# Ninety-seven half-width operand sums on GpSimd instead of VectorE, in a kernel that is planned instruction by instruction

## The chip, the cores and the metric

The kernel runs on one core of a Trainium2 chip. The metric is device time in microseconds (us). The kernel before was timed three times: 1730.5, 1730.49 and 1730.0 us, with a median of 1730.49 us.

The core has a TensorE (PE in the profile, and PEld for its weight loads), a VectorE (DVE), a ScalarE (ACT), a GpSimd (POOL) and a SyncE (SP). In this kernel SP issues nearly all loads, and POOL issues nearly all stores and all transfers that add to what is already at their destination.

## The reference

Two branches are computed from inputs of 2048 rows and mixed by a gate that has one value for each row:

```python
g = sigmoid((x * gate_w).sum(-1, keepdims=True))           # x: 2048 x 1024
a = einsum("bsd,ed->bse", x, dft_hid_re)                   # 1024 x 1024 matrices
b = einsum("bsd,ed->bse", x, dft_hid_im)
A = einsum("ts,bse->bte", dft_seq_re, a) - einsum("ts,bse->bte", dft_seq_im, b)   # 2048 x 2048 matrices
h = einsum("bsd,df->bsf", x, w1) + b1                      # 1024 -> 3584
r = where(h > 0, h, 0); r = r * r
B = einsum("bsf,fd->bsd", r, w2) + b2                      # 3584 -> 1024
out = g * A + (1 - g) * B
```

Everything is 32-bit floating point. The kernel takes `A_x` as the x of both branches, as the reference does.

## The kernel before

**Stages.** The work is five matrix products in order: the x stage (x with the two hidden matrices, giving a and b, called `ab`), the c stage (the two sequence matrices with `ab`, giving the first branch, times the gate), two h stages (x with the two parts of w1, then bias, relu and square), and the o stage (the squares with w2, bias, gate and the sum of both branches). What goes from one stage to the next is stored to device memory and loaded again.

**Fewer products.** Each product is split into 2 x 2 blocks and formed by the Winograd scheme: seven block products in place of eight, at the price of sums of blocks. The sums are listed in `SUMS_L` and `SUMS_R` (S1 to S4 of the left, T1 to T4 of the right operand, lines 63 to 77). For the block products named in `TWICE_X`, `TWICE_C`, `TWICE_O` and `TWICE_H` the scheme is applied a second time. The sums of operands are tiles called `raw` (made in the place of a loaded block) or `sum`; tiles called `u`, `y`, `h`, `ab` and `o` hold results. Block results are combined from PSUM, mostly by VectorE instructions that read one operand from PSUM (`ps`).

**Precision.** Each operand is split into a high part `hi`, which ScalarE makes by a copy to TensorE's reduced 32-bit type, and a low part `lo`, which VectorE makes by subtraction. Each pair of tiles is multiplied three times: hi with hi, hi with lo, lo with hi. A tile named `both` holds the two parts of a narrow operand side by side. For operands marked in `MINUS_C` and `MINUS_O` ScalarE makes a negated copy instead, and an adding DMA from POOL makes `lo` of it.

**Sums by DMA.** For some sums, chosen by the `LAND_...`, `LAND2_...` and `APART_...` tables, the second block is added to the first by an adding DMA, so that VectorE does nothing. `SHARE2`, `MADE`, `LOW` and `HIGH` say which sums, low parts and high parts are stored to be loaded by a later use, `EARLY_...` and `NOW_...` which are made ahead of their use, `NOT_OUT` which outputs of the first branch are kept aside and not written to the output at once.

**The planner.** Nothing is issued while the kernel is described. Every instruction is recorded as an `Op` (line 134) with the engine, the operands and a modelled time, for instance `VEC[0] + VEC[1] * n` for VectorE. `plan` (line 1458) then plays the program on modelled engines and queues. The matmuls have a fixed order. Every other instruction has a due time, worked back from the matmul that needs it, and whenever a modelled engine is idle, it takes the instruction that is due first among those whose inputs are there. A tile gets one of 55 slots when its turn comes; the turn is its due time less a lead, `LEAD` and `LEADS`, where `LEADS` is a table of corrections for each 25 us of the program. `emit` (line 1610) issues everything in the order so found, and ties the instructions of each engine to that order; so all instructions stand under line 1628 of the profile, and they are told apart by their tiles' names. Waits between engines follow from the data. An `Op` can also have a `gate`, an instruction whose end it has to wait for though it needs nothing from it; before the change only some DMAs of POOL have one (lines 1566 to 1571).

The heart of the choice, for any engine other than TensorE (lines 1562 to 1564):

```python
                if not ready[e]:
                    continue
                op = ready[e][0][2]
```

## Time and profile before

| | |
|---|---|
| median of three runs | 1730.49 us |
| span of the profiled execution, first to last instruction | 1727.9 us |
| what lies around the span, against the median | 2.6 us |
| TensorE busy, instructions | 1722.6 us (100%), 8024 |
| TensorE weight loads busy | 1508.7 us (87%), 8024 |
| VectorE busy, instructions | 1658.3 us (96%), 1659 |
| ScalarE busy, instructions | 1151.2 us (67%), 1296 |
| GpSimd busy, instructions | 284.3 us (16%), 413 |
| moved by DMA | 559.89 MB |
| DMA engines' time taken by SP's and ACT's packets, by POOL's packets | 52.9%, 44.4% |

The profile is of one execution. A row of a group gives the line, the engine, the operation, the tile written and those read, the shapes and the count; then the busy time in us and the mean of one in ns; then the idle time ahead of the group and what ended most of it. In rows of the timeline the first number is the start, the second the length, in us. In rows of waits stand the total, the number of times and the longest. POOL's busy time before the change is the issuing of DMAs, with four small memsets at the start.

### The profile page before, as it was taken

To read this page: it belongs to the slowest core of one execution; us is meant where nothing else is said; L and a number is where in the kernel's file an instruction comes from. 1 tells how busy PE (TensorE), PEld (TensorE's weight loads), DVE (VectorE), ACT (ScalarE), POOL (GpSimd) and SP (SyncE) were. 2 spreads that over 40 slices of the span, in tenths; PEclk is the share of its full clock that TensorE was granted. 3 is DMA by queue.
4 is the path that set the end of the run, shared out by engine and by line. 5 is a ranking of instruction groups with operands and counts; after the bars stand their busy time and mean duration, and the time that the engine had idled before them with its cause. 6 is when DMAs were issued, how large, how long until landed. Compare 5 with 4: busy or idle time off the path is not lost.

```text
span 1727.9 us, 22479 instructions
## 1 busy us (share of the span) xinstructions
PE 1722.6 (100%) x8024; PEld 1508.7 (87%) x8024; DVE 1658.3 (96%) x1659; ACT 1151.2 (67%) x1296; POOL 284.3 (16%) x413
## 2 busy tenths in 40 slices
PE   9999999999999999999999999999999999999999
PEld 8888888888888888888888888888888888888888
DVE  7999999999999899899999999999999999899997
ACT  5475565874675675466595668987897666476673
POOL 1212221111211100121121210101211120111131
PEclk9999999999999999999999999999999999999999
DMA  9996999999999999998998999999999999999997
GB/s 347 365 375 259 322 387 343 292 285 327 285 307 352 291 310 399 323 295 285 371 359 311 276 355 344 351 379 358 309 345 324 336 272 381 341 277 334 334 295 162
DMA packets 157807, 559.89 MB, mean 324 GB/s; under 512 B 17776, under 2 KB 18304, under 8 KB 157696
## 3 DMA queue, kind: packets, MB, share of 16 engines
q1 hardware_dynamic: 98352, 351.07, 52.9%
q0 software_dynamic: 58912, 207.00, 44.4%
q8 instruction: 63, 1.03, 0.2%
q10 hardware_dynamic: 432, 0.39, 0.1%
q14 instruction: 48, 0.39, 0.1%
HBM read 390.09 MB, written 134.75 MB: 304 GB/s over the span
## 4 chain that ended last, share of the span: by engine, by line
PE 96%; DVE 3%; DMA 1%; issue 0%; ACT 0%; DVEq 0%; POOLq 0%
PE ps L1628 96%; DVE lo L1628 1%; DVE sum L1628 1%; DMA raw<-in_w1a 1%; DVE y L1628 0%; DVE both L1628 0%; DVE u L1628 0%; DVE raw L1628 0%; ACT hi L1628 0%; ACT y L1628 0%; DVE o L1628 0%; ACT both L1628 0%; ACT ps L1628 0%; DVE ones L1628 0%; DVEq L1628 0%
## 5 line engine op out<-in xcount | busy, mean ns | idle before, releaser
L1628 PE MATMUL ps<-hi,lo 128*128 128x512 f32 (+1 forms) x2100 | 730.4, 378 | 0.1
L1628 PE MATMUL ps<-hi 128*128 128x512 f32 (+1 forms) x2100 | 730.4, 378 | 0.0
L1628 PE MATMUL ps<-lo,hi 128*128 128x512 f32 (+1 forms) x2100 | 730.3, 378 | 0.0
L1628 ACT ACTIVATE hi<-raw 128x1024 fp32r<-128x1024 f32 (+2 forms) x397 | 401.5, 1032 | 200.2 <-DVE raw L1628 79.6
L1628 PEld LDWEIGHTS ps<-hi,lo 128*128 128x128 f32 x2100 | 396.6, 189 | 56.5 <-DVE lo L1628 0.7
L1628 PEld LDWEIGHTS ps<-lo,hi 128*128 128x128 f32 x2100 | 396.7, 189 | 56.1 <-DVE lo L1628 0.2
L1628 PEld LDWEIGHTS ps<-hi 128*128 128x128 f32 x2100 | 396.6, 189 | 56.0 <-ACT hi L1628 0.2
L1628 DVE TENSOR_TENSOR lo<-raw,hi 128x1024 fp32r<-128x1024 f32 (+2 forms) x337 | 396.0, 1192 | 14.2 <-ACT hi L1628 10.8
L1628 ACT ACTIVATE hi<-sum 128x1024 fp32r<-128x1024 f32 (+1 forms) x263 | 269.1, 1032 | 136.7 <-DVE sum L1628 88.1
L1628 PE MATMUL ps<-hi,both 128*128 128x512 f32 x1120 | 312.3, 379 | 0.0
L1628 DVE TENSOR_TENSOR lo<-sum,hi 128x1024 fp32r<-128x1024 f32 (+1 forms) x230 | 270.5, 1191 | 8.7 <-PE ps L1628 4.6
L1628 PEld LDWEIGHTS ps<-hi,both 128*128 128x128 f32 x1120 | 211.7, 189 | 30.2 <-ACT ps L1628 0.2
L1628 DVE TENSOR_TENSOR raw<-raw 128x1024 f32<-128x1024 f32 (+1 forms) x175 | 205.7, 1195 | 1.6 <-DMA raw<-in_ct 0.5
L1628 DVE TENSOR_TENSOR sum<-raw 128x1024 f32<-128x1024 f32 (+2 forms) x182 | 180.5, 1002 | 7.9 <-PE ps L1628 4.4
L1628 PE MATMUL ps<-lo,both 128*128 128x512 f32 x560 | 182.9, 379 | 0.0
L1628 DVE TENSOR_TENSOR sum<-raw,sum 128x1024 f32<-128x1024 f32 (+2 forms) x139 | 147.6, 1066 | 4.4 <-DMA raw<-copy 2.1
L1628 ACT ACTIVATE u<-ps 128x1024 f32<-128x1024 f32 (+1 forms) x91 | 88.1, 970 | 47.5 <-PE ps L1628 28.0
L1628 PEld LDWEIGHTS ps<-lo,both 128*128 128x128 f32 x560 | 105.8, 189 | 15.0
L1628 ACT ACTIVATE ps<-u 128x1024 f32<-128x1024 f32 (+1 forms) x69 | 67.8, 987 | 21.9 <-DVE u L1628 9.5
L1628 POOL DMA_DIRECT2D h<-h x58 | 31.3, 542 | 250.5 <-ACT h L1628 91.0
L1628 POOL DMA_DIRECT2D lo<-raw x38 | 34.0, 896 | 224.9 <-ACT lo L1628 172.1
L1628 ACT ACTIVATE both<-sum 128x512 fp32r<-128x512 f32 x68 | 42.3, 622 | 35.9 <-DVE sum L1628 33.7
(87 smaller groups left out, 1140.0 us busy)
## 6 DMA issues: line engine op xcount, KB each, us to landing
raw<-in_ct SPq DMA_DIRECT2D x137, 512.0 KB, 10.1
raw<-h SPq DMA_DIRECT2D x99, 512.0 KB, 10.5
raw<-in_w SPq DMA_DIRECT2D x90, 512.0 KB, 10.3
raw<-ab SPq DMA_DIRECT2D x72, 512.0 KB, 10.9
raw<-copy SPq DMA_DIRECT2D x65, 512.0 KB, 7.8
raw<-in_x SPq DMA_DIRECT2D x56, 512.0 KB, 8.4
copy<-raw POOLq DMA_DIRECT2D x48, 512.0 KB, 6.9
h<-h POOLq DMA_DIRECT2D x44, 512.0 KB, 6.6
```

What stands on the lines that cost most here:

```text
L1628: made = getattr(real[op.engine], op.name)(*(actual(a) for a in op.args), **{k: actual(v) for k, v in op.kwargs.items()})
```

## The change

Of the operand sums that VectorE would make, 97 half-width ones (128 x 512) are issued on GpSimd. A sum that is 512 wide goes as a whole. A sum that is 1024 wide is cut into two halves; one goes to GpSimd, the other is left to VectorE, or goes to GpSimd at a later occasion.

Which sums go is decided in `plan`. VectorE's ready instructions are kept in two heaps: those with more than one operand in SBUF (and `tensor_scalar`), flagged `two`, and the others, in `single`, which are mostly those that read PSUM. Whenever VectorE begins one of the `single` kind, `beside` looks for a sum to be put on GpSimd at that moment. It wants GpSimd idle, no POOL instruction ready that is due within 2 us, an instruction on VectorE about as long as the modelled sum (0.1 + 2.2e-3 x 512 us), and a sum whose inputs have all landed and which is due 3 us later or more. While the sum runs in the model, VectorE is given `single` instructions only. The sum gets a `gate`: the VectorE instruction just before the covering one, or the one ahead of that where the three follow each other without a pause.

Besides, the plan is made anew: the tables that say which sums are landed by DMA, kept, shared or made early have other entries, and `LEADS` has corrections in nearly every window. The tables of products (`TWICE_...`, `WIDE`, `TALL_...`, `FIRST_...`, `SPILL`) are the same, written on lines of their own.

```diff
-LAND_X, LAND_C, LAND_H, LAND_O = {'T1': 3, 'T3': 4, 'T4': 3}, {'T1': 15, 'T3': 0, 'T4': 13}, ({'T1': 0, 'T3': 4, 'T4': 3}, {'T1': 0, 'T3': 1, 'T4': 1}), {'T1': 10, 'T3': 3, 'T4': 9}
+LAND_X = {'T1': 2, 'T3': 1, 'T4': 3}
+LAND_C = {'T1': 16, 'T3': 1, 'T4': 14}
+LAND_H = ({'T1': 0, 'T3': 4, 'T4': 4}, {'T1': 0, 'T3': 1, 'T4': 3})
+LAND_O = {'T1': 10, 'T3': 3, 'T4': 9}
...
+LAND2_C = {1: {'T1': 0}, 2: {'T1': 4, 'T3': 2}, 3: {'T3': 1}, 4: {'T1': 2, 'T3': 2}, 5: {'T1': 1}, 6: {'T1': 1, 'T3': 2}, 7: {'T1': 1, 'T3': 3}}
+LAND2_O = {1: {'T1': 1, 'T3': 0}, 2: {'T1': 1}, 3: {'T3': 4, 'T1': 1}, 4: {'T3': 1}, 5: {'T1': 3, 'T3': 2}, 6: {'T1': 3}, 7: {'T1': 3, 'T3': 4}}
...
+BESIDE = (0.1, 2.2e-3, 0.05)
+BESIDE_LEAD = 3.0
+BESIDE_OVER = 0.15
+BESIDE_DMA = 2.0
...
+            near = [a for a in args[1:] if isinstance(a, Sight) and a.base.home != "bank" and a.size() >= 256]
+            self.two = engine == "vector" and (len(near) > 1 or name == "tensor_scalar")
+            self.moves = (name == "tensor_tensor" and len(near) == 2 and outs[0].base.name in ("raw", "sum")
+                          and n in (512, 1024))
...
+    single, port, recent = [], [0.0], deque([None, None], 2)
+
     def able(op):
         if op.engine != "tensor":
-            heappush(ready[op.engine], (op.due, op.at, op))
+            heappush(single if op.engine == "vector" and not op.two else ready[op.engine], (op.due, op.at, op))
+
+    def beside(t, op):
+
+        room = op.time + BESIDE_OVER
+        if (idle["gpsimd"] > t + 1e-9 or port[0] > t + 1e-9 or BESIDE[0] + BESIDE[1] * 512 > room
+                or ready["gpsimd"] and ready["gpsimd"][0][0] < t + BESIDE_DMA):
+            return
+        e = min((e for e in ready["vector"] if e[2].moves and not e[2].unlanded and e[0] >= t + BESIDE_LEAD),
+                key=lambda e: e[:2], default=None)
+        if e is None:
+            return
+        ready["vector"].remove(e)
+        heapify(ready["vector"])
+        o, time = e[2], BESIDE[0] + BESIDE[1] * 512
+        if o.whole:
+            part = o
+            part.engine, part.time = "gpsimd", time
+        else:
+            o.parts, o.moved, o.start = 2 if o.n == 1024 else 1, True, t
+            part = Beside(o, 0 if o.n == 1024 else None, "gpsimd", time, VEC_END)
+            if o.n == 1024:
+                heappush(ready["vector"], (o.due, o.at, Beside(o, 1, "vector", VEC[0] + VEC[1] * 512, VEC_END)))
+        last, before = recent[1], recent[0]
+        part.gate = before if last and before and last.start - before.start < before.time + 1e-6 and (
+            op.start - last.start < last.time + 1e-6) else last
+        part.start = t
+        order.append(part)
+        idle["gpsimd"], port[0] = t + time, t + time + BESIDE[2]
...
+            elif e == "vector":
+                heaps = [h for h in ((single,) if port[0] > t + 1e-9 else (ready[e], single)) if h]
...
+            if e == "vector":
+                if not op.two:
+                    beside(t, op)
+                recent.append(op)
```

## The prediction

> **What bounds the kernel now.** I read the page first, then how the matmuls follow each other, then what TensorE's weight loads waited for, and only then VectorE, whose work the change takes away. From the page, the span, the engines, the granted clock and the chain of waits by engine:

> ```profile
> span 1727.9 us, 22479 instructions
> PE 1722.6 (100%) x8024; PEld 1508.7 (87%) x8024; DVE 1658.3 (96%) x1659; ACT 1151.2 (67%) x1296; POOL 284.3 (16%) x413
> PEclk9999999999999999999999999999999999999999
> PE 96%; DVE 3%; DMA 1%; issue 0%; ACT 0%; DVEq 0%; POOLq 0%
> ```

> TensorE is busy for the whole span at its full granted clock, and the chain that ended last is 96% TensorE. Its busy time alone proves little, since matmuls overlap; their starts prove more. Two places of the timeline, the first real matmuls and a run near the end, with the last matmul and the work after it:

> ```profile
> 5.69 0.70 PE L1628 MATMUL ps<-hi 128*128 128x512 f32 x2
> ...
> 1718.41 0.38 PE L1628 MATMUL ps<-hi 128*128 128x512 f32 x1
> ...
> 1720.57 0.38 PE L1628 MATMUL ps<-lo,hi 128*128 128x512 f32 x1
> ...
> 1723.57 0.28 PE L1628 MATMUL ps<-hi,lo 128*128 128x256 f32 x1
> 1723.88 0.48 DVE L1628 SCALAR_TENSOR_TENSOR o<-ps,b2c,g 128x256 f32<-128x256 f32 x1 [0.34 <-PE ps L1628]
> 1724.40 0.43 DVE L1628 TENSOR_TENSOR o<-o,raw 128x256 f32<-128x256 f32 x1
> ```

> From 1718.41 to 1720.57 lie ten starts: 0.216 us each. Of the 8024 matmuls 44 are the warm-up of the code, so 7980 are real, nearly all of them 512 wide. They start between 5.69 and 1723.57 us: 1717.9 us, 0.2153 us for each, which is the pace itself. So there is hardly a hole. The waits of the weight loads say how large the holes are:

> ```profile
> PEld ps L1628 <- DVE lo L1628: 0.9, 3, 0.5
> PEld ps L1628 <- ACT ps L1628: 0.2, 1, 0.2
> PEld ps L1628 <- ACT hi L1628: 0.2, 1, 0.2
> ```

> Together 1.3 us in the whole run. The span is 5.7 us of start, 1717.9 us of matmuls and 4.3 us of tail; 1.3 us of it is waiting. VectorE, at 96%, looks like a second bound, and in some stretches it has no idle time at all:

> ```profile
> 850.00:900.00 50.00, 50.00 (x233) 43.78 (x232) 49.93 (x45) 38.44 (x46) 10.80 (x21) 1.00 0.95 364
> 900.00:950.00 50.00, 50.00 (x234) 43.77 (x233) 50.00 (x45) 28.58 (x29) 7.32 (x13) 1.00 0.89 327
> 950.00:1000.00 50.00, 50.00 (x233) 43.80 (x232) 50.00 (x45) 35.73 (x43) 14.16 (x21) 1.00 0.98 290
> 1000.00:1050.00 50.00, 50.00 (x233) 43.77 (x233) 50.00 (x46) 28.52 (x32) 3.06 (x6) 1.00 0.99 358
> ```

> The columns are the stretch, its length, busy time (with the count) of PE, PEld, DVE, ACT and POOL, the clock, the DMA share and GB/s. Over these 200 us VectorE is busy for 199.93, and yet TensorE starts as many matmuls as anywhere: VectorE works ahead of need. Its load is full without being late.

> **The change part by part.** *The matmuls.* The diff leaves alone which products are formed one level or two levels deep, their orders and the tile shapes, so the 7980 matmuls and their 1717.9 us stay. What the change can give back is at most the 1.3 us of waits: 0 to 1.3 us, and I take 0.2, since nothing says that the three waits on `lo` come from sums.

> *Sums taken from VectorE.* The rows by form of the sums and of the instructions that are to cover them:

> ```profile
> L1628 DVE TENSOR_TENSOR raw<-raw 128x1024 f32<-128x1024 f32 x160 | 191.4, 1218 | 1.6 <-DMA raw<-in_ct 0.5 <-DMA raw<-in_w 0.5 <-DMA raw<-ab 0.2
> L1628 DVE TENSOR_TENSOR sum<-raw 128x512 f32<-128x512 f32 x68 | 46.4, 685 | 3.9 <-PE ps L1628 3.6
> L1628 DVE TENSOR_TENSOR lo<-raw,hi 128x1024 fp32r<-128x1024 f32 x310 | 372.7, 1219 | 9.2 <-ACT hi L1628 5.9 <-PE ps L1628 2.4
> L1628 DVE TENSOR_TENSOR u<-u,ps 128x1024 f32<-128x1024 f32 x45 | 54.5, 1215 | 2.0 <-ACT u L1628 1.0 <-PE ps L1628 0.3
> L1628 DVE TENSOR_TENSOR h<-h,ps 128x1024 f32<-128x1024 f32 x43 | 52.2, 1214 | 1.2 <-PE ps L1628 1.0
> L1628 DVE TENSOR_TENSOR ab<-ab,ps 128x1024 f32<-128x1024 f32 x41 | 49.7, 1215 | 2.6 <-PE ps L1628 1.4 <-ACT u L1628 1.2
> ```

> A sum that is 512 wide leaves VectorE whole: 0.685 us. Of a 1024-wide one VectorE keeps a half: 1.218 - 0.685 = 0.533 us saved. For 97 halves that is 97 x 0.533 = 52 to 97 x 0.685 = 66 us; I take 60. Covers there are enough: the last three rows alone hold 129 full-width instructions that read PSUM, for 97 sums.

> *The same sums on GpSimd.* No GpSimd arithmetic is in this trace, so its price is bounded. It isn't below VectorE's own 0.685 us for that size. As the upper bound I take twice VectorE's full-width row, 2.44 us. The longest kind of instruction that GpSimd issues now is the first row here:

> ```profile
> L1628 POOL DMA_DIRECT2D out<-o x15 | 16.7, 1202 | 44.5 <-DVE o L1628 12.5 <-ACT lo L1628 11.9 <-DVE lo L1628 6.6
> L1628 POOL DMA_DIRECT2D lo<-raw x38 | 34.0, 896 | 224.9 <-ACT lo L1628 172.1 <-DVE lo L1628 19.9 <-DVE u L1628 18.0
> ```

> Between the ends I take 1.2 us, by that nearest row and because the planner puts a sum beside one full-width instruction (1.215 us). Then POOL gets 97 x 1.2 = 116 us more and is busy for 400 of 1728 us, 23%; with 2.44 us it would be 521 us, 30%. It doesn't become a bound. [...]

> *What a sum collides with.* While a sum runs over the end of its cover, the next VectorE instruction may have to wait. Nothing in this trace shows how much: POOL issued DMAs all through, and VectorE's two-SBUF-input rows (1.218 and 1.219 us) are as long as those that read PSUM (1.214 and 1.215 us), so issuing doesn't hurt it, but issuing isn't arithmetic. From below nothing, from above each sum stops VectorE for its whole 1.2 us: 116 us. I take a quarter of it, 0.3 us for each sum, 29 us, because the start of each sum hangs on a semaphore of VectorE and is off by parts of a microsecond and not by whole instructions. [...]

> *What planning anew moves.* By the tables of the diff: four fewer sums of the first stage are landed by adding DMAs (+4 VectorE instructions), three more of the second stage are (-3); one level deeper three fewer there and five more in the last stage (+3, -5); `lo` made by a negated copy and an adding DMA in five more places and in two fewer (-5, +2). That is about -4 instructions of 1.22 us. The other tables (kept operands, sums and outputs kept far, early sums) I bound by ten instructions either way: -5 us, from -17 to +7. As many adding DMAs of 0.9 us come to or leave POOL. VectorE thus ends at 1658 - 60 + 29 - 5 = 1622 us, with bounds of 1575 and 1729: only at the upper end does it become the bound.

> *Queues.* The 97 sums stand in order in POOL's queue between its some 409 DMA issues; each also waits there for its cover's turn. The issue behind it is late by at most that wait and the sum, 1.2 + 1.2 = 2.4 us. What waits for these issues are `lo<-raw` and landings, which took about 9 us before and are asked for well ahead. SP's queue gets loads in another order at the same sizes. At nothing these are costed because of the slack that the full stretches above show; without it each would be a wait of TensorE.

> The sum: 5.7 + 1717.9 + 4.3 - 0.2 = 1727.7 us of span. The median of the runs, 1730.49 us, lies 2.6 us above the profiled span; with that, **1730.3 us**. Other arithmetic at the new places may leave a wait here or there; its own range is 1729.2 to 1732.

> **The rivals.** *Contention makes VectorE the bound* (slower). Mechanism: a sum overhangs its cover and holds up VectorE's next instruction for 1.2 us while only 0.53 to 0.69 was saved, a net loss of about 0.6. It decides where VectorE has no idle time: 200 us out of 1728 hold about 11 of 97 sums, 11 x 0.6 = 7 us lost, and TensorE stands once the lead is spent. Time: 1737. For it: the full stretches. Against it: only overhangs count, and those stretches run without any wait now.

> *POOL's DMAs come late* (slower). The one larger hole now, at the change of stage, shows the mechanism; the chain of waits there:

> ```profile
> 815.91 9.39 DMA raw<-in_w1a
> 825.30 0.02 issue
> 825.32 1.06 ACT hi L1628
> 826.38 0.02 issue
> 826.41 1.24 DVE lo L1628
> 827.64 0.04 issue
> 827.69 896.17 PE ps L1628 x4174
> ```

> A transfer issued at 815.91 landed 9.39 us later, and the operand was ready 12 us after the issue, just too late. Where POOL issues such a transfer behind a sum it comes 2.4 us later; two such places without slack cost 4.8 us: 1735.3. It decides from the second such place on.

> *The change does not relieve VectorE* (it waits as long as it saves): 1730.5, since TensorE doesn't need the relief.

> [...]

> *Faster by over 0.2%* would need 3.5 us, and the waits are 1.3; only start and tail could give the rest, and no edit makes their work smaller.

> **How the numbers follow.** What a measurement tells from no change is 0.2%, 3.5 us, so 1727.0 to 1733.9 counts as the same. Chances: the forecast 0.64; no relief 0.07; first-use cost 0.03 (all the same: 0.74); POOL late 0.14 and contention 0.10 (slower: 0.24); faster 0.02. The range goes from 1729.2, below which only a shorter start could lie, up to 1737.0, the priced end of both slower cases; beyond it I leave about 0.1.

> **What would show it.** Right: the same 7980 matmuls at 0.216 us, waits of the weight loads of 0 to 3 us in sum, VectorE's busy time near 1622 us, POOL's near 400, and sum rows on POOL of about 1.2 us. Contention right: means of VectorE's two-input rows above 1.25 us. POOL late: weight loads that wait for `lo` or `hi` behind a DMA that POOL issued. The prediction is wrong if the weight loads' waits sum to over 4 us, or if the matmuls' pace is another.

## The result, and the profile after

The changed kernel takes **1742.63 us** (median of four runs, 1739.05 to 1743.09) against 1730.3 us before (median of four runs, one more than when the prediction was made): 1.0068 of the time, 95% interval 1.0054 to 1.0081. It is slower by 12.3 us, where 1730.3 us was forecast, and it lies 5.6 us above the upper end of the range. The profiled execution is the shortest of the four (1739.05 us, span 1737.3); the size of the waits differs from one execution to the next, as a second profile below shows.

From the page of the kernel after, the span, the engines, the granted clock and the chain of waits by engine:

```profile
span 1737.3 us, 22640 instructions
...
PE 1724.2 (99%) x8024; PEld 1507.6 (87%) x8024; DVE 1616.1 (93%) x1619; ACT 1148.8 (66%) x1293; POOL 445.5 (26%) x510
...
PEclk9999999999999999999999999999999999999999
...
PE 77%; DVE 3%; DMA 2%; issue 1%; ACT 1%; POOL 0%; DVEq 0%; ACTq 0%; POOLq 0%
```

VectorE did lose its work: 1658.3 us became 1616.1. The matmuls are the same 8024. What changed is the last line: TensorE's share of the chain that sets the end fell from 96% to 77%, and no other engine took it over as a bound. The chain is now broken in many places. What the weight loads waited for, kernel after (total, times, longest; a start-up row left out):

```profile
PEld ps L1741 <- DVE ab L1741: 5.3, 4, 2.3
PEld ps L1741 <- ACT ps L1741: 3.3, 5, 1.2
PEld ps L1741 <- DMA lo<-raw: 2.2, 1, 2.2
...
PEld ps L1741 <- ACT hi L1741: 0.6, 1, 0.6
PEld ps L1741 <- DVE lo L1741: 0.2, 1, 0.2
```

Together 11.6 us in twelve waits, where it was 1.3 us in five. The span grew by 9.4 us, the waits by 10.3: in the profiled execution the waits are the whole loss, to within a microsecond. GpSimd is in none of the rows. So the next question is what made VectorE, ScalarE and the adding transfer late. VectorE's own waits, kernel after:

```profile
DVE raw L1741 <- DMA raw<-in_x: 11.3, 3, 4.5
DVE sum L1741 <- DMA raw<-copy: 9.3, 5, 2.8
...
DVE raw L1741 <- DMA raw<-in_w: 5.9, 3, 3.1
```

and the largest rows of the same kind in the kernel before:

```profile
DVE sum L1628 <- DMA raw<-copy: 3.1, 4, 1.8
...
DVE sum L1628 <- DMA raw<-in_x: 1.2, 1, 1.2
```

Over all its rows VectorE waited 51.2 us for transfers after, and 6.5 us before. It has 42 us less to do and yet is later where it counts, because what it is to work on isn't there.

**One place, followed back.** The timeline of after around the first of the larger waits, from POOL's transfers to TensorE (start, length; in brackets the idle time before and what ended it):

```profile
28.54 0.85 POOL L1741 DMA_DIRECT2D raw<-in_w  x1 [8.40 <-ACT hi L1741]
...
32.10 5.33 SPq L1741 DMA_DIRECT2D raw<-in_x  x4
...
32.78 0.83 POOL L1741 DMA_DIRECT2D lo<-lo  x1
...
43.35 1.23 DVE L1741 TENSOR_TENSOR raw<-raw 128x1024 f32<-128x1024 f32 x1 [4.45 <-DMA raw<-in_x]
49.38 1.22 DVE L1741 TENSOR_TENSOR raw<-raw 128x1024 f32<-128x1024 f32 x1 [3.67 <-DMA raw<-in_x]
...
57.49 2.18 POOL L1741 TENSOR_TENSOR sum<-raw 128x512 f32<-128x512 f32 x1 [1.50 <-DVE ab L1741]
58.47 1.21 DVE L1741 TENSOR_TENSOR ab<-u,ps 128x1024 f32<-128x1024 f32 x1
...
59.74 0.48 PE L1741 MATMUL ps<-hi 128*128 128x512 f32 x1 [1.89 <-DVE ab L1741]
```

Between 28.54 and 32.78 us POOL issues eight transfers in a row (before, two in the same 5 us and the next ones at 35.91 us and later). SP's loads of x are issued into that. The first, issued at 32.10, landed at 40.75: 8.66 us, where the planner had reckoned with 6.92. The second, whose landing at 43.27 ended VectorE's first wait, took 10.75 us (planner: 9.19), and the fourth, whose landing at 49.26 ended its second wait, 12.62 us (planner: 11.49); the first and the fourth were also issued 1.4 us later than planned. POOL's eight, on the other hand, landed up to 2.9 us sooner than planned. VectorE stood 4.45 and then 3.67 us, got to `ab` late, and TensorE, which needs the PSUM bank that `ab` frees, stood 2.3 us. The first sum on GpSimd starts at 57.49, when VectorE's waits are over and the last matmul ahead of the hole has started (57.47): at this place the sums can't be the cause. In the last stage the chain of waits of after shows the same kind of thing (start, length):

```profile
1468.30 0.55 POOL copy L1741
1468.85 0.64 issue
1469.50 11.95 DMA lo<-raw
1481.50 76.29 PE ps L1741 x352
```

An adding transfer took 11.95 us (planner: 9.39) and the matmuls waited for its landing.

### The profile page after: what moved, and what is told of

It reads as the page before. It is cut to its first block, busy times and chain, and to the rows that moved or that the text cites. A ratio compares the mean times of both kernels' runs of the same rounds, so it can differ in the third digit from the quotient of the medians.

```text
span 1737.3 us, 22640 instructions
## 1 busy us (share of the span) xinstructions
PE 1724.2 (99%) x8024; PEld 1507.6 (87%) x8024; DVE 1616.1 (93%) x1619; ACT 1148.8 (66%) x1293; POOL 445.5 (26%) x510
## 4 chain that ended last, share of the span: by engine, by line
PE 77%; DVE 3%; DMA 2%; issue 1%; ACT 1%; POOL 0%; DVEq 0%; ACTq 0%; POOLq 0%
PE ps L1741 77%; DVE lo L1741 1%; DMA raw<-h 1%; DMA lo<-raw 1%; DVE raw L1741 1%; DVE u L1741 1%; DVE o L1741 1%; DVE sum L1741 0%; DMA raw<-in_w 0%; ACT ps L1741 0%; ACT hi L1741 0%; DVE both L1741 0%; ACT o L1741 0%; DVE y L1741 0%; DVE ab L1741 0%
## 5 line engine op out<-in xcount | busy, mean ns | idle before, releaser
L1741 ACT ACTIVATE hi<-raw 128x1024 fp32r<-128x1024 f32 (+2 forms) x401 | 406.3, 1032 | 193.7 <-DVE raw L1741 66.6
L1741 DVE TENSOR_TENSOR lo<-raw,hi 128x1024 fp32r<-128x1024 f32 (+2 forms) x340 | 400.5, 1192 | 24.3 <-ACT hi L1741 16.1
L1741 ACT ACTIVATE hi<-sum 128x1024 fp32r<-128x1024 f32 (+1 forms) x260 | 264.1, 1031 | 114.0 <-DVE sum L1741 62.8
L1741 DVE TENSOR_TENSOR raw<-raw 128x1024 f32<-128x1024 f32 (+2 forms) x165 | 189.5, 1159 | 27.1 <-DMA raw<-in_x 11.3
L1741 DVE TENSOR_TENSOR sum<-raw 128x512 f32<-128x512 f32 (+2 forms) x166 | 158.7, 965 | 13.9 <-DMA raw<-copy 6.8
L1741 DVE TENSOR_TENSOR sum<-raw,sum 128x1024 f32<-128x1024 f32 (+2 forms) x121 | 127.6, 1057 | 9.2 <-DMA raw<-copy 2.5
L1741 POOL TENSOR_TENSOR sum<-raw 128x512 f32<-128x512 f32 x37 | 65.8, 1778 | 101.9 <-DVE lo L1741 39.3
L1741 POOL TENSOR_TENSOR raw<-raw 128x512 f32<-128x512 f32 x33 | 54.1, 1638 | 113.0 <-DVE lo L1741 52.4
```

What stands on the lines that cost most here:

```text
L1741: made = getattr(real[op.engine], op.name)(*(actual(a) for a in op.args), **{k: actual(v) for k, v in op.kwargs.items()})
```

## The experiments

Two theories at first. **S**: the sums on GpSimd cost the time themselves, by holding up VectorE or POOL's queue. **P**: the new order of the instructions, which came with the other tables and with the planner that knows of the sums, is what loses. All ratios are to the kernel before, measured on the same chip (the first row is from the chip of after; on the others its median was 1729.7 to 1730.0 us). The waits are those of one profiled execution, which for after is the shortest of four and for after_lead the longest.

| kernel | median us | ratio, 95% interval | weight loads' waits, us (times) | VectorE's waits for DMA, us |
|---|---|---|---|---|
| before | 1730.3 | | 1.3 (5) | 6.5 |
| after | 1742.63 | 1.0068 (1.0054 to 1.0081) | 11.6 (12) | 51.2 |
| narrow_sums | 1739.85 | 1.0058 (1.0043 to 1.0073) | 8.4 (7) | 44.3 |
| extra_sums | 1729.88 | 1.0001 (0.9992 to 1.0010) | 1.0 (4) | 7.5 |
| new_order | 1740.12 | 1.0054 (1.0040 to 1.0069) | 8.2 (10) | 14.0 |
| no_sums | 1764.17 | 1.0200 (1.0183 to 1.0217) | 34.3 (34) | 28.8 |
| small_adds | 1733.85 | 1.0021 (1.0012 to 1.0031) | 4.7 (6) | 18.8 |
| old_tables | 1736.47 | 1.0037 (1.0024 to 1.0050) | 8.4 (10) | 34.3 |
| same_order | 1729.29 | 0.9997 (0.9988 to 1.0005) | 0.6 (2) | 10.4 |
| after_again | 1743.50 | 1.0078 (1.0062 to 1.0093) | 14.8 (11) | 46.7 |
| after_lead | 1750.47 | 1.0129 (1.0104 to 1.0154) | 23.9 (17) | 45.0 |
| old_leads | 1739.65 | 1.0067 (1.0050 to 1.0083) | 11.0 (15) | 37.8 |
| few_loads | 1729.69 | 1.0000 (0.9991 to 1.0009) | 2.3 (6) | 12.2 |
| more_loads | 1730.62 | 1.0006 (0.9997 to 1.0016) | 1.8 (7) | 11.2 |

The planner also gives its own account of how long it expects TensorE to stand; where that is used below it is called the account.

**narrow_sums: after's order, most of each sum left out.**

```diff
+            if op.engine == "gpsimd" and op.name == "tensor_tensor":
+                if op.outs[0].base.name == "sum":
+                    tc.nc.gpsimd.memset(args[0][..., 16:], 0.0)
+                args = [a[..., :16] for a in args]
```

> Changed kernel, same order of every engine, but each of the 97 GpSimd sums adds 16 columns and not 512 (where the sum's tile is new, the other columns are filled with zeros by GpSimd); so most of each sum is left out. Theory S (the sums themselves cost the time: their length, the collisions with VectorE and the delay of POOL's queue): the waits of the weight loads fall from 11.6 us to 3 or less, 1731 us, at most 1733. Theory P (the order that was planned anew leaves too little room where transfers land later than the planner assumed, and the sums have little to do with it): the same places of waiting, 1737 us or more.

Measured: 1739.85 us. A sum shrank to about a third, and the waits stayed. With the zeros that fill the rest of 64 new tiles (35 us), GpSimd's work for the sums fell from 166 to 96 us. The largest group of sums on POOL, and then the waits of the weight loads:

```profile
L1746 POOL TENSOR_TENSOR raw<-raw 128x16 f32<-128x16 f32 x33 | 19.0, 575 | 134.1 <-DVE lo L1746 61.3 <-DVE sum L1746 23.8 <-DVE u L1746 20.6
```

```profile
PEld ps L1746 <- ACT ps L1746: 3.3, 4, 1.4
PEld ps L1746 <- DVE ab L1746: 2.9, 2, 2.4
PEld ps L1746 <- DMA lo<-raw: 2.2, 1, 2.2
```

Of the 12.3 us some 2 to 3 came back, no more than the intervals of the two ratios leave open. Of after's three largest waits those near 58 and 1479 us stand as they stood. The third, 1.8 us near 273 us, where VectorE has no pause, fell to 0.5: about 1 us there goes with the sums. The rest speaks for P.

**extra_sums: before's order, with useless sums.** 151 sums of 320 columns on a tile that nothing else reads, each beside a VectorE instruction that reads PSUM.

```diff
+            made = tc.nc.gpsimd.tensor_tensor(extra, extra, extra, op=ADD)   # waits like a sum with a gate
```

> Kernel before, order untouched, with 151 useless sums of 320 columns on GpSimd (as many elements as 94 of 512), each beside a VectorE instruction that reads PSUM and gated as in the change. VectorE loses nothing and gains nothing but the collisions. Theory S: 1736 us or more. Theory P: 1730 to 1732.

Measured: 1729.88 us, no change. The page's engines, and the group on POOL:

```profile
PE 1722.3 (100%) x8024; PEld 1508.5 (87%) x8024; DVE 1659.5 (96%) x1660; ACT 1151.9 (67%) x1296; POOL 486.2 (28%) x564
```

```profile
L1667 POOL TENSOR_TENSOR extra<-extra 128x320 f32<-128x320 f32 x151 | 203.9, 1351 | 324.0 <-DVE lo L1651 131.0 <-DVE sum L1651 73.2 <-DVE raw L1651 39.0
```

204 us of arithmetic on GpSimd, more than the 166 us of the real sums, cost VectorE 1.2 us of busy time (1658.3 before, 1659.5 here) and TensorE nothing. Placed beside VectorE instructions that read PSUM, these 151 sums held up hardly anything; in before's order S has no mechanism left.

**new_order: before, planned anew, no sums at all.** One number of the planner's leads is other, so that the order is another while the work is the same.

```diff
-LEAD = {'hi': 2.2, 'out': 1.4, 'raw': 6.7, 'sum': 10.0}
+LEAD = {'hi': 2.5, 'out': 1.4, 'raw': 6.7, 'sum': 10.0}
```

> Kernel before, no sum on GpSimd, planned with a lead of 2.5 us in place of 2.2 for the tiles of high parts: nothing but the order of instructions and the slots differ from 468 us on. By the planner's own account its last matmul ends 1.6 us later than before. Theory S: 1730 to 1733, as the planner has it. Theory P (a new order meets late transfers that the old one happened to avoid): 1735 to 1742.

Measured: 1740.12 us, as slow as after, without one sum on GpSimd. But here the account says so itself: 7.2 us of standing against 8.2 measured. Before is the odd one: its account says 5.6, and the chip shows 1.3. So an order under the old tables need only do what its account says to lose several us against before. After's order has an account of zero and stands for 11.6 us; "any new order loses" is not yet the answer for it.

**no_sums: after's tables and planner, nothing moved.** `beside` returns at once.

```diff
     def beside(t, op):
+        return
```

> Changed kernel with its new tables, but no sum is moved to GpSimd: VectorE makes all of them. By the planner's own account TensorE then stands for 24.7 us, where with the sums moved it has 0. Theory S: the sums cost 9 us on the chip and save much less than planned, so 1745 or less. Theory P: the sums' relief is real under these tables and the new order's own 9 us come on top, 1750 to 1760.

Measured: 1764.17 us, with 34.3 us of waits; VectorE is busy for 1660.5 us. That is 4 us above P's range. Under the new tables the sums on GpSimd, with the order that goes with them, are thus worth 21.5 us. The relief is real where the plan needs it; before's plan doesn't.

**small_adds: after's order, adding transfers of a quarter of the columns.** It leaves all else in place, and takes 64 of 560 MB away.

```diff
+        if op.load and "accum_op" in op.kwargs:
+            args = [a[..., :a.shape[-1] // 4] for a in args]
```

> Changed kernel, same order of every engine and all 97 sums whole, but every adding DMA moves a quarter of its columns, so three quarters of these additions are left out. Transfers land earlier: these and the loads that share the DMA engines with them. Theory P (late landings stop TensorE): the waits of the weight loads fall from 11.6 us to 3 or less, 1731 to 1733 us. Against it, a theory O (the order is bad in itself, VectorE and ScalarE meet their due times too late whatever lands when): 1737 us or more.

Measured: 1733.85 us and 4.7 us of waits, close to P's range (1731 to 1733, 3 us or less) but outside it. Waits of the weight loads:

```profile
PEld ps L1744 <- DVE ab L1744: 3.0, 4, 1.3
...
PEld ps L1744 <- ACT hi L1744: 0.9, 1, 0.9
PEld ps L1744 <- DMA lo<-raw: 0.8, 1, 0.8
```

By the ratios some 8 of the 12 us came back by nothing but lighter transfers, with all 97 sums in full. After's loss hangs on when transfers land. It doesn't follow that they land later there than in before: in small_adds SP's loads take on average 3.4 us less than the planner reckons, sooner than in either kernel.

**old_tables: after's planner and sums (87 of them), before's tables and leads.**

```diff
-LAND_X = {'T1': 2, 'T3': 1, 'T4': 3}
+LAND_X = {'T1': 3, 'T3': 4, 'T4': 3}
...
```

> The changed planner, so sums go to GpSimd, with all tables and leads of the kernel before: the part of the change that is the sums alone (87 of them by its plan). The planner's own account ends the matmuls 3.7 us later than that of the kernel before. Theory P: a new order, so slower than its account, 1735 to 1743. Theory S (already weak): the sums' own price, 1740 or more.

Measured: 1736.47 us and 8.4 us of waits, against an account of 9.3. Under the old tables new_order and this run do what the planner says, without sums and with them.

**same_order: before's order and tables, and 57 sums moved in place.** The first halves of 40 sums 1024 wide and 17 whole ones 512 wide go to GpSimd behind a cover; nothing else is moved.

```diff
+LEAST = 1.2
...
-    for op in order:
+    for op in beside(order):     # 40 Half pieces and 17 whole sums are issued on GpSimd, with a gate
```

> The kernel before with its tables and its order kept, and 57 of its operand sums moved to GpSimd beside VectorE's instructions that read PSUM, gated as in the change: 40 halves of 1024-wide sums and 17 whole ones of 512, chosen among those whose inputs land early enough. Everything else keeps its place. Theory P: 1729 to 1731, since nothing lands later and VectorE wasn't the bound; VectorE's busy time falls by 40 x 0.53 + 17 x 0.69 = 33 us to about 1626. Theory S: 1734 or more. If relief of VectorE alone were worth time: 1728 or less.

Measured: 1729.29 us, the same time within 0.2%. The page's engines, and the weight loads' waits:

```profile
PE 1722.3 (100%) x8024; PEld 1509.0 (87%) x8024; DVE 1637.5 (95%) x1642; ACT 1150.7 (67%) x1296; POOL 387.3 (22%) x470
```

```profile
PEld ps L1674 <- ACT hi L1674: 0.4, 1, 0.4
PEld ps L1674 <- ACT ps L1674: 0.2, 1, 0.2
```

VectorE loses 20.8 us, where 33 were expected; nine of its instructions that begin inside a sum are longer, by 5.6 us in all, and the rest of the difference isn't explained. The waits fall to 0.6, and there is no more to gain, because there was no more than 1.3 us of waiting. This is what the forecast described, minus the planning anew.

**stalls_long and stalls_short: what a wait of TensorE costs.** In before's order, sums on GpSimd hold one matmul back: 8 places with three chained sums, or 16 with one.

```diff
+PLACES, SUMS = 8, 3          # stalls_short: 16, 1
...
+            tc.add_manual_dep(made.ins, idle.ins.name, ...)   # the matmul waits for the last sum
```

> Kernel before, order untouched; at 8 places, some 190 us apart and with POOL idle, one matmul waits for three chained GpSimd sums of 320 columns, which begin when the matmul ahead of it ends: 8 waits of some 3 us. If a wait costs its own length and no more: 1730 + 24 = 1754. If the granted clock is halved after such a wait, as it was for 3.4 us after a wait of 2.2 us in the kernel with narrow sums: up to 1.7 to 3.4 us more for each, 1760 to 1780.

> The same with 16 places and one sum at each: 16 waits of some 1.2 us. With or without a rule of the clock, if it asks for a longer wait than this: 1730 + 19 = 1749, and no stretch at half clock. If waits of 1.2 us are enough to halve the clock: 1755 or more.

Measured: 1788.17 us (1.0348, interval 1.0316 to 1.0381) and 1786.49 us (1.0335, 1.0302 to 1.0368), for these waits, stalls_long first and stalls_short below:

```profile
PEld ps L1643 <- POOL extra L1649: 43.3, 8, 8.5
```

```profile
PEld ps L1643 <- POOL extra L1649: 48.2, 16, 9.1
```

The waits came out longer than meant, 43.3 us for 24 and 48.2 us for 19, so both times lie above the sums of the expectations; that stalls_short passed 1755 us doesn't mean that waits of 1.2 us halve the clock. 58 us lost for 43 us of waits, 56 for 48: in these two runs nothing of the waits was made good, and 15 and 8 us were lost on top of them. What those are is in the last section.

**after_again, after_lead, old_leads: is only the fitted order off?** Two forms of P are left. **Y**: under the new tables transfers land later than the planner reckons, whatever the order. **Z**: only the one order that was fitted until its account came to zero is off, having been chosen for the planner's mistakes. The first run repeats after; the second gives it the lead of new_order; the third gives it before's table `LEADS` (99 sums).

```diff
-LEAD = {'hi': 2.2, 'out': 1.4, 'raw': 6.7, 'sum': 10.0}
+LEAD = {'hi': 2.5, 'out': 1.4, 'raw': 6.7, 'sum': 10.0}       # after_lead
-LEADS = {'hi': {0: -1.5, 1: -6.0, ...
+LEADS = {'hi': {3: -5.5, 4: -4.5, ...                         # old_leads
```

> The changed kernel once more. Its profiled run took 1739.05 us and its timed runs 1742.2 to 1743.1. If the difference is a stretch at half the granted clock behind the wait of 2.3 us near 58 us: a run of 1742 to 1743 has 6.8 us of half clock in its records (3.4 us lost), one of 1739 has none. If it is something else: the clock is whole in both.

> Changed kernel, planned with a lead of 2.5 us in place of 2.2 for the tiles of high parts: its tables, another order, 90 sums moved. By the planner's own account TensorE stands for 12.2 us (the changed kernel: 0). Theory Z (the account is about right for an order that wasn't fitted to it, and too good for the one that was): waits of the weight loads of 9 to 16 us, 1739 to 1748 us with some half clock. Theory Y (under the new tables transfers land late whatever the order, 11 us beyond the account): 20 us of waits or more, 1750 or more.

> Changed kernel with its new tables, but with the table of corrections of leads of the kernel before; 99 sums moved. By the planner's own account TensorE stands for 6.2 us. Theory Z: waits of 4 to 10 us, 1734 to 1741 us. Theory Y: 16 us of waits or more, 1746 or more.

Measured waits less the account: after 11.6 - 0, after_lead 23.9 - 12.2 = 11.7, no_sums 34.3 - 24.7 = 9.6, old_leads 11.0 - 6.2 = 4.8. With the old tables: before 1.3 - 5.6 = -4.3, new_order 8.2 - 7.2 = 1.0, old_tables 8.4 - 9.3 = -0.9. Four orders with the new tables stand 5 to 12 us longer than reckoned, three with the old ones not. So the loss goes with the new tables, and not with the one fitted order alone. Between Y and Z the two runs don't decide: after_lead is at Y's edge (1750.47 us, and its 23.9 us are those of an execution of 1758.94), old_leads is in Z's range by its time and 1 us above it by its waits.

Y's reason isn't borne out. Set against the planner's own times, SP's loads took on average 0.78 us less than planned in after and 0.85 us less in before. The slowest twentieth took at least 1.6 us more than planned in after, 1.3 in before, and 1.7 in old_tables, whose waits equal its account. Transfers miss their planned times by much the same in all three; what the new tables seem to leave is less room for it. That is inferred, and no run measures the room by itself.

after_again shows how the same program varies: its waits came to 14.8 us. Neither of the two expectations came true as worded. The wait near 58 us, 2.2 us, was again not followed by half clock; another, at 1570 us, was, for 3.41 us. That is 1.7 of the 5.1 us between the two profiled executions, and the rest is longer waits.

**few_loads and more_loads: are the DMA engines as a whole out of slack?** In before the packets of both large queues take 97.3% of 16 engines' span, so that could have been why a new order has nowhere to put its transfers (theory D), as against single places that are ill placed (theory L).

```diff
+LOADS = 26                   # more_loads: 52
...
+            made = tc.nc.sync.dma_start(tc.extra, tc.xn[0][:, :320])
```

> The kernel before, in its own order, with 26 useless loads of 128 x 320 numbers (160 KB each, 4.3 MB in all, 0.8% of the 560 MB that it moves), issued by SyncE behind every so many of its own loads, some 60 us apart, into a tile that nothing reads. In the profile of before the packets of both large queues take 97.3% of 16 engines' span, 1681 us for 560 MB, 3.0 us for each MB; so the loads cost about 13 us of DMA time, and 1727.9 - 1681 = 47 us are idle, start and tail among them. Open question: is a late landing a wait of TensorE because the DMA engines as a whole have no slack (theory D), or are only single places of the new order ill placed, while the DMA engines have slack on the whole (theory L)? D: the weight loads' waits grow by 4 to 13 us and the time to 1734 to 1743, VectorE waits for DMAs rather over 15 us than 6.5. L: 1730 to 1732, waits under 3 us.

> The same with 52 loads, some 30 us apart (8.5 MB, 1.5%; about 26 us of DMA time of the 47 that are idle). D: the time grows by about twice as much as with 26 loads, to 1738 to 1756, waits of the weight loads 9 to 26 us. L: 1730 to 1733, waits under 4 us.

Measured: 1729.69 and 1730.62 us, both the same time as before. The queue of more_loads, and its weight loads' waits:

```profile
q1 hardware_dynamic: 105840, 359.60, 54.4%
```

```profile
PEld ps L1632 <- ACT ps L1632: 1.0, 3, 0.6
PEld ps L1632 <- DVE lo L1632: 0.6, 3, 0.2
PEld ps L1632 <- ACT hi L1632: 0.2, 1, 0.2
```

8.5 MB more, and TensorE's waits are 1.8 us instead of 1.3. VectorE's waits for transfers grew by some 5 us in each, and its lead took them up. D falls: 97% was no limit, since 1.5% more bytes cost no time that can be measured, and the old order has slack where it is needed. What after lacks, then, is slack at single places.

## Why the prediction was wrong, point by point

**The step that failed** is the one on queues and planning anew: "At nothing these are costed because of the slack that the full stretches above show; without it each would be a wait of TensorE." The full stretches show the slack of the old order. The change issues another order, and of that the profile of before shows nothing. The slack is a property of the plan that ran; that it would carry over to a plan made anew had no row behind it. The conditional half of the sentence came true: there were twelve waits, 11.6 us, well over the 4 us that the prediction gave as its own sign of being wrong. I had read the line of the diff about `LEADS` and the tables as "about -4 instructions of 1.22 us", a sum over work; what they change is when each transfer is issued.

- *Matmuls, 1717.9 us unchanged*: right, the same 8024 instructions, and in the profiled execution of after the clock was granted in full up to the last matmul.
- *At most 1.3 us to gain*: right; same_order took 57 sums away and stayed within 0.2%, and extra_sums had no effect either.
- *VectorE at 1622 us*: right, 1616.1, by parts that were off and cancel. The tables were put at -5 us; no_sums, where nothing else changes VectorE's work, shows +2 (1660.5). The count left out `LAND_H`, by which three more sums are landed, and it took three more `lo` for made by adding DMAs, where the traces have 60 and had 64. The sums and their collisions were put at -60 + 29 = -31 us and came to -44: the collisions are about 8 us, not 29. The 0.3 us for each sum was the author's estimate; after shows 0.08 us.
- *A sum of 1.2 us*: near what a sum takes that meets nothing (1.27 to 1.30 us), too small for the mean. From after's groups:

```profile
L1741 POOL TENSOR_TENSOR sum<-raw 128x512 f32<-128x512 f32 x37 | 65.8, 1778 | 101.9 <-DVE lo L1741 39.3 <-PE ps L1741 16.7 <-DVE sum L1741 15.1
L1741 POOL TENSOR_TENSOR raw<-raw 128x512 f32<-128x512 f32 x33 | 54.1, 1638 | 113.0 <-DVE lo L1741 52.4 <-DVE sum L1741 20.2 <-DVE u L1741 18.6
```

  The means of 1.64 to 1.78 us mix two kinds. The 35 sums that take 1.27 to 1.30 us all start outside of any VectorE instruction with two SBUF inputs; 37 sums of 1.9 to 2.3 us all start inside one, and end on average 1.15 us behind it; most of the others also start inside one, late in it. POOL came to 445.5 us, against 400.
- *The collisions*: it happens the other way round as well: 27 VectorE instructions with two SBUF inputs that start inside a sum, 0.18 us or more ahead of its end, are longer than others of their size. Timeline of after:

```profile
224.60 1.50 POOL L1741 TENSOR_TENSOR raw<-raw 128x512 f32<-128x512 f32 x1 [7.75 <-DMA raw<-in_w]
...
224.88 2.30 DVE L1741 TENSOR_TENSOR sum<-sum,raw 128x1024 f32<-128x1024 f32 x1
```

  This one took 2.30 us, where the mean is 1.22, and ended 1.08 us behind the sum; the 27 are 7.7 us longer in all. The effect is small because mostly the sum is second, and in after's rows of waits neither TensorE nor VectorE waits for a sum; ScalarE does eight times, 23.5 us in all.
- *Rival "contention makes VectorE the bound"*: out. VectorE is less busy, and extra_sums with half as many sums again costs nothing.
- *Rival "POOL's DMAs come late"*: the nearest. The two places followed back above do go back to late transfers, and small_adds speaks for it at the others. Its sign, a wait for `lo` or `hi` behind POOL's DMA, is met by one wait, 2.2 of the 11.6 us. But its cause was a sum ahead of an issue in POOL's queue, 2.4 us at two places; narrow_sums, with sums of 0.6 us, still has 8.4 us of waits, and what leads to the first larger wait comes before the first sum. It is the order, at most of some eight places. The exception is the wait near 273 us: with the sums short it falls from 1.8 to 0.5 us, with the adding transfers light only to 1.3.
- *Rival "first use"*: out; the first sum takes 2.18 us, of which the first 1.05 lie inside a VectorE instruction with two SBUF inputs, and that is the length of the later sums that start inside one (1.9 to 2.3 us). No run shows a cost of the first.
- *The range*: its upper end was "the priced end of both slower cases", with 0.1 left beyond it. A price for an order without slack wasn't in it. The row for one was quoted, the transfer of 9.39 us that came just too late at the change of stage; I counted two such places and had no reason for two.

**What stays open**: which entries of the new tables take the room away. At the first place eight transfers of POOL run beside the loads of x; that they are the cause is argued from their times and not shown. With lighter adding transfers the waits near 60 us fall from 2.7 to 0.8 us, though few of these eight add. A run with only these eight made lighter was not tried. Nor is it known why before stands for 4.3 us less than its account. No kernel here beats the one before by more than can be measured.

## What to carry to other kernels

Before pricing what an edit saves on an engine, add up what the bounding engine waits for: with 1.3 us of waits in 1728, no relief of another engine can be worth more, however full that engine is. When an edit comes with a new plan, the new order is the larger part of it: a profile shows the slack of the order that ran, not of the next one, and here two other orders under the old tables cost 6 and 10 us. A plan's own account isn't a forecast: it put the change 5.6 us ahead of before, and the chip puts it 12 us behind. Zero waits in the model say nothing of the margin for a transfer that lands 2 us late; look at where transfers bunch, and put such an edit first into the order that is known to run well.

## What the runs showed of the hardware that had not been expected

```profile
58.00:60.00 2.00, 0.05 (x1) 0.00 (x0) 2.00 (x4) 0.00 (x0) 1.80 (x2) 1.00 1.01 406
60.00:62.00 2.00, 1.96 (x7) 1.61 (x8) 2.00 (x4) 1.31 (x2) 0.00 (x0) 0.74 1.04 422
62.00:64.00 2.00, 2.00 (x6) 1.61 (x5) 2.00 (x2) 0.69 (x1) 1.04 (x1) 0.50 1.09 307
64.00:66.00 2.00, 2.00 (x10) 1.72 (x9) 1.38 (x3) 0.06 (x1) 0.68 (x2) 0.91 1.03 281
```

In stalls_short the waits are of many lengths. Two of them, timeline: the first holds a matmul back from 198.60 to 199.90, and the second from about 706.8 (the last of the three) to 709.14:

```profile
198.60 0.38 PE L1643 MATMUL ps<-lo,hi 128*128 128x512 f32 x1
...
199.90 0.48 PE L1643 MATMUL ps<-hi,lo 128*128 128x512 f32 x1 [0.92 <-POOL extra L1649]
...
706.40 0.81 PE L1643 MATMUL ps<-hi,lo 128*128 128x512 f32 x3
709.14 2.28 PE L1643 MATMUL ps<-hi,lo 128*128 128x512 f32 x5 [1.93 <-POOL extra L1649]
```

and the window behind the second:

```profile
710.00:712.00 2.00, 2.00 (x6) 1.62 (x5) 2.00 (x3) 0.66 (x1) 0.00 (x0) 0.50 1.04 414
```

Matmuls then started 0.427 us apart instead of 0.216. Measured from start to start, the nine gaps of 1.3 to 1.8 us in stalls_short never had this, one of 2.3 us had it, one of 2.5 us hadn't, and all from 3.26 us on had it, as had all eight of stalls_long (3.1 to 8.5 us). Gaps of 2.2 to 2.3 us in after and new_order hadn't, and one of 2.2 us in no_sums had. The stretch of narrow_sums lasted 3.41 us, and so did the one behind the second wait above; at the matmuls' halved pace 3.41 us lose 1.7. In stalls_short a gap of 3.26 us, up to 1314.39, had a longer one:

```profile
1310.91 0.59 PE L1643 MATMUL ps<-hi,both 128*128 128x512 f32 x2
1314.39 0.79 PE L1643 MATMUL ps<-lo,both 128*128 128x512 f32 x1 [2.88 <-POOL extra L1649]
```

```profile
1313.00:1315.00 2.00, 0.61 (x2) 0.52 (x3) 0.76 (x1) 2.00 (x3) 1.33 (x1) 0.64 1.02 416
1315.00:1317.00 2.00, 2.00 (x6) 1.62 (x5) 0.00 (x0) 2.00 (x4) 0.00 (x0) 0.50 1.08 317
1317.00:1319.00 2.00, 2.00 (x6) 1.53 (x6) 0.72 (x1) 0.82 (x1) 0.00 (x0) 0.50 1.00 238
1319.00:1321.00 2.00, 2.00 (x8) 1.63 (x7) 1.63 (x2) 0.00 (x0) 0.00 (x0) 0.65 0.84 285
```

It lasted 6.83 us, from 1313.56 on; 0.83 us of it lie within the wait, and the other 6.0 lose 3.0. In stalls_long the sum comes out: 41 us of gaps and half of the 32 us at half clock behind them make the 57 us that its profiled execution is longer than before. The shortest gap with half clock behind it was one of 2.2 us, the longest without one of 2.5. In the profiled execution of after no gap between matmuls is longer than 2.3 us and no clock was lost up to the last of them; in after_again one wait had grown to 3.3 us and was followed by a stretch of 3.41 us:

```profile
1571.00:1574.00 3.00, 3.00 (x9) 2.32 (x9) 3.00 (x4) 3.00 (x4) 0.00 (x0) 0.52 0.93 224
```

So waits near this length are one source of the spread of after's runs, and longer waits are the larger one.
